# Loads of queries, keys and values one step later and in several pieces, with five buffers of attention outputs

## The chip, the cores and the metric

The kernel runs on one core of a Trainium2 chip. The metric is the device time of one execution in microseconds (us): lower is better. The time before is the median of three runs, 1153.46 us (1153.4 to 1158.42). The engines have their usual short names: PE is TensorE (matmul; PEld its weight loads), DVE is VectorE, ACT is ScalarE, POOL is GpSimd, SP is SyncE. SP computes nothing here: it issues DMA transfers, one after the other, in the order of the program.

## The reference

Two layers follow one another. The first is attention over 8 sequences of 576 positions with 8 heads of 64; each head sees only a causal band. Four heads see the last 32 positions, four see every fourth of the last 128. The second is a mixture of 8 experts over the 4608 tokens, of which each token takes the two with the highest noisy gate logits.

```
mask_plain = (rel >= 0) & (rel < window)
mask_dil = (rel >= 0) & (rel < window * dilation) & (rel % dilation == 0)
...
attn = attn / (np.sum(attn, axis=-1, keepdims=True) + 1e-09)
return np.matmul(attn, v)
...
noisy_logits = logits + noise_scale * noise
top2 = np.argpartition(-noisy_logits, 2, axis=1)[:, :2]
...
    h = np.maximum(x[mask] @ w1[e], 0.0)
    out[mask] += top2_w[mask, k, None] * (h @ w2[e])
```

All of it is float32. In the kernel the expert products are made of three matmuls on values that are split into a high and a low part.

## The kernel before, in words

**Attention.** The work is cut into 8 groups: four pairs of sequences, and for each pair first the four dilated heads, then the four plain ones. A group has three steps, so there are 24 steps (k = 0 to 23), and group g holds steps 3g, 3g+1 and 3g+2. The loop over i (line 879) is a software pipeline: in pass i it emits the scores of step i (`qk`), the exponential and the transpose of step i-1 (`expo`, `ptr`), the stores and transposes of the outputs of step i-2 (`store_x`, `x_transpose`), the product with the values of step i-1 (`pv`) and the gate matmuls of step i-2 (`gate_mm`).

`qk` needs the keys `KT` and queries `QT` of its group; `pv` needs its values, `VD` for dilated heads and `VP[0]`, `VP[1]` for plain ones. There is one set of these buffers for the dilated and one for the plain heads. The loads of group g+1's values can thus go out when group g-1 has used its own, those of group g+2's keys and queries when group g has.

`pv` ends in a VectorE multiply (line 354) that writes the normalized output `x` of its step, one of three buffers. `store_x` writes it to the scratch tensor `xs` in HBM with six DMAs (lines 365 and 367), from where the experts' gathers fetch it. A buffer of `x` can be written again when the stores that read it have landed.

**Order.** The order on each queue is that of the program text; nothing is reordered on the chip. What has no fixed place in the loop is hung into numbered slots: `at(kb, f)` puts `f` into slot kb, and pass i works off slot 2i (`fillers`, before `store_x`) and slot 2i+1 (after `pv` and `gate_mm`). So the lines that the change touches, 783 to 790, say behind which stores on SP's queue each load stands. Before, the values of group g+1 go to slots 6g+1 and 6g+2, and keys and queries of group g+2 to slot 6g+5, each tensor in one DMA. `VD` is loaded in three DMAs, `VP` in two, one for each sequence.

Other things that SP issues in these slots: two fills of the table `tab` (line 236, slots 6 and 12; it waits for VectorE), clears of the output (line 860, from slot 38 on), the loads of the first expert's w1 (line 565, from slot 41 on) and, for the first expert, small loads of the list of its tokens (line 611), which VectorE copies at line 627. The gate's selection (`gate`) is a generator that is worked off a few instructions at a time.

**Experts.** After the loop come the experts. For each, the tokens' rows are gathered from `xs` by GpSimd (line 643 or 650), transposed, split, and multiplied by w1 (line 697) and w2 (line 738); GpSimd adds the weighted rows to the output (line 715). Weights are staged through two buffers `ws` and split by ScalarE and VectorE (lines 573 to 588). Here `plan` places loads and splits by a reckoned time of TensorE. The first loads of w2 (line 579) are due at once, so they follow the last attention stores on SP's queue, and ScalarE splits the first piece (line 586) between the evictions of the first expert's hidden layer (line 701).

Of the kernel before, what the change touches and what calls it, by code (L numbers as in the profile page):

```python
# [9 lines left out]
F32 = mybir.dt.float32  # L10
# [35 lines left out]
def attention_moe_kernel(ctx, tc, qt, kp, kd, vpl, vdl, w_gate, w_noise, noise, w1, w2, out, CAP=1216, SPLITS=(0, 384, 896)):  # L46
# [25 lines left out]
    sm = actx.enter_context(tc.tile_pool(name="sm", bufs=2))  # L72
# [20 lines left out]
    def qk_loads(g, parts=1):  # L93
        u, ty = g // 2, 1 - g % 2
        for i in range(parts):
            for dst, src in ((KT[ty], (kp, kd)[ty][u]), (QT[ty], qt[u, ty])):
                n = dst.shape[1] // parts
                yield lambda d=dst[:, n * i:n * i + n], s=src[:, n * i:n * i + n]: sync.dma_start(d, s)

    def v_loads(g):  # L100
        u, ty = g // 2, 1 - g % 2
        if ty:
            d = VD.rearrange("p j h y c -> p (j h y c)")
            n = d.shape[1] // 3
            for i in range(3):
                yield lambda i=i: sync.dma_start(d[:, n * i:n * i + n], vdl[u, :, n * i:n * i + n])
        else:
            for b in range(2):
                yield lambda b=b: sync.dma_start(VP[b].rearrange("p j h c -> p (j h c)"), vpl[u, b])
# [138 lines left out]
    def micro(n=1):  # L248

        n = (1, n, 2 * n)[rate[0]]
        for g in list(gens):
            while n > 0 and g not in held:
                try:
                    r = next(g)
                except StopIteration:
                    gens.remove(g)
                    break
                n -= 1  # L260
                if r == 2:
                    room[0] -= 1
                if r == 1 or room[0] <= 0:
                    held.add(g)
                if r == 3:
                    break
# [6 lines left out]
    def blocks(st, ty):  # L273

        for r in range(6):
            for w in range(2):
                a, jp = divmod(r, 3)
                if ty == 0:
                    b, ub = divmod(12 * st + 2 * r + w, 18)
                else:  # L280
                    b, ub = divmod(6 * st + 2 * jp + w, 9)
                yield r, w, a, jp, b, ub
# [47 lines left out]
    def pv(k):  # L330
        g, st = divmod(k, 3)
        ty = 1 - g % 2
        pt = PT.pop(k)
        o = aps.tile([128, 2, 512], F32, name="o", tag="o")
        for hh in range(4):
            for r, w, a, jp, b, ub in blocks(st, ty):
                qd, c0 = (r, hh) if r < 4 else (2 * (r - 4) + hh // 2, 4 + hh % 2)
                if ty == 0:
                    y, src = hh // 2, 2 * (hh % 2) + a
                    rhs = VP[b][64 * w:64 * w + 64, ub // 2, hh]  # L340
                else:
                    y, src = a, hh
                    rhs = VD[64 * w:64 * w + 64, 3 * st + jp, hh, y]
                tensor.matmul(o[32 * qd:32 * qd + 32, w, 65 * c0:65 * c0 + 65],
                              lhsT=pt[64 * w:64 * w + 64, y, 128 * jp + 32 * src:128 * jp + 32 * src + 32],
                              rhs=rhs, start=True, stop=True, skip_group_check=True)
        ov = o[:, :, 0:390].rearrange("p w (c d) -> p w c d", d=65)
        x = sm.tile([128, 2, 6, 64], F32, name="x", bufs=3)
        den = sm.tile([128, 2, 6], F32, name="den")
        vector.tensor_scalar(den, ov[:, :, :, 64], 1e-9, None, op0=OP.add)  # L350
        micro(1)
        vector.reciprocal(den, den)
        micro(1)
        vector.tensor_tensor(x, ov[:, :, :, 0:64], den.unsqueeze(3).to_broadcast([128, 2, 6, 64]), op=OP.mult)
        XG[k] = x
# [408 lines left out]
    def plan(t, f, lag=None):  # L764

        if lag is not None:
            plan(t, lambda: plan(now[0] + lag, f()))
        else:
            heappush(due, (t, next(turn), f))
# [9 lines left out]
    def at(kb, *fs):  # L779
        fill.setdefault(kb, []).extend(fs)  # L780

    NK = 12 * U
    for g in range(2 * U):
        s0 = 6 * g
        if g + 1 < 2 * U:
            for i, f in enumerate(v_loads(g + 1)):
                at(s0 + 1 + i // 2, f)
        if g + 2 < 2 * U:
            for f in qk_loads(g + 2):
                at(s0 + 5, f)  # L790
    for u in range(U):
        for st in range(3):
            if (u, st) != (U - 1, 2):
# [67 lines left out]

    places = [*range(SL_ZERO, NK + 5)]
    for i in range(NZERO):
# [15 lines left out]
    for i in range(NS + 2):  # L879
        slot[0] = 2 * i  # L880
        early[0] = True
        micro(2)
        early[0] = False
        if i < NS:
            qk(i)
        micro(2)
        if 1 <= i <= NS:
            expo(i - 1)
        micro(2)
        if 1 <= i <= NS:  # L890
            ptr(i - 1)
        micro(2)
        micro(2)
        fillers(2 * i)
        if i >= 2:
            store_x(i - 2)
            x_transpose(i - 2)
        micro(2)
        if 1 <= i <= NS:
            pv(i - 1)  # L900
        micro(2)
        if i >= 2:
            gate_mm(i - 2)
        micro(2)
        micro(2)
        fillers(2 * i + 1)
# [24 lines left out]
    for kb in sorted(fill):  # L931
        for f in fill.pop(kb):
            plan(2.0 * (kb - NK - 5), f)
    start = 0.0
# [135 lines left out]
```

## Time and profile before

| what | value |
|---|---|
| median of 3 runs | 1153.46 us |
| profiled execution, its time | 1155.89 us |
| profiled execution, span from first to last instruction | 1154.2 us |
| TensorE busy (matmul) | 1023.6 us, 89% of the span |
| VectorE, ScalarE, GpSimd busy | 468.6, 289.4, 509.3 us |
| mean granted TensorE clock | 0.950 |
| last score matmul, last `pv` multiply | 243.0 us, 261.5 us |
| first and last store of `xs` | 18.8 us, 272.3 us |

The page cuts the span into 40 slices of 28.9 us. Attention fills the first nine of them. A row of a timeline gives the start, the duration, the engine (SPq is SP's queue), the line, the operation and the number of instructions merged into the row; in square brackets the engine's idle time ahead of it and what ended that. A DMA instruction's duration on SPq is the time until SP could hand it over, not that of the transfer. A row of waits gives the engine and line that waited, for what, and then the sum, the count and the longest, in us. A row of windows gives the busy time and instruction count of each of the five engines, the granted clock, the share of time in which the core's 16 DMA engines were busy, and what they moved in GB/s.

### The profile page before, as it was taken

How to read it: one execution, taken by the hardware profiler on the slowest of the kernel's cores; microseconds unless marked ns; L12 is line 12 of the kernel's file. 1: busy time of each engine (PE TensorE's matmuls, PEld its weight loads, DVE VectorE, ACT ScalarE, POOL GpSimd, SP SyncE). 2: the span in 40 equal slices, each digit the busy share in tenths (PEclk: the TensorE clock that was granted, in tenths of full speed). 3: DMA queues.
4: the chain of work that ended last, by engine and by line, in shares of the span. 5: the costliest groups of instructions: out<-in, count | busy, mean ns of one | idle time of the engine just before them, and what ended most of it. 6: DMA issues, size and time to landing. Idle time of an engine off the chain costs nothing. (4 is left out here: it accounts for less than half of the span.)

```text
span 1154.2 us, 22635 instructions
## 1 busy us (share of the span) xinstructions
PE 1023.6 (89%) x9630; PEld 870.0 (75%) x9631; DVE 468.6 (41%) x1043; ACT 289.4 (25%) x540; POOL 509.3 (44%) x620
## 2 busy tenths in 40 slices
PE   6765766455889999999999999999999999999996
PEld 4554545345669878897988899888978888998895
DVE  5544353444424454334433543444343335423221
ACT  1433332252212231213122322222231223212110
POOL 3000623242836676357534654463566256542112
PEclk8898877778999999999999999999999999999998
DMA  9665555655633443434342434333343524343123
GB/s 341 233 220 189 179 190 206 198 184 177 204 71 60 117 103 92 78 80 112 75 109 49 116 62 112 85 89 73 85 109 72 111 51 112 63 112 73 19 28 43
DMA packets 78538, 135.07 MB, mean 117 GB/s; under 512 B 29168, under 2 KB 41504, under 8 KB 75616
## 3 DMA queue, kind: packets, MB, share of 16 engines
q1 hardware_dynamic: 55520, 93.22, 24.5%
q0 software_dynamic: 22912, 40.35, 19.4%
q8 instruction: 77, 1.26, 0.4%
q14 instruction: 29, 0.24, 0.1%
HBM read 92.72 MB, written 40.81 MB: 116 GB/s over the span
## 5 line engine op out<-in xcount | busy, mean ns | idle before, releaser
L697 PE MATMUL up<-x,w1h 128*128 128x512 f32 (+2 forms) x1536 | 408.7, 350 | 0.0
L650 POOL DMA_INDIRECT g<-xs,ixi x266 | 266.3, 1001 | 94.7 <-issue 76.2
L697 PEld LDWEIGHTS up<-x,w1h 128*128 128x128 f32 x1536 | 276.8, 189 | 24.5 <-DVE hl L702 0.2
L697 PE MATMUL up<-x,w1l 128*128 128x384 f32 (+2 forms) x768 | 267.6, 348 | 0.0
L715 POOL DMA_INDIRECT out_rows<-y,ixs x70 | 112.1, 1602 | 311.3 <-DVE y L747 279.4
L738 PE MATMUL dn<-w2h,hh 128*128 128x512 f32 x576 | 225.3, 391 | 1.2 <-DVE y L747 1.2
L738 PE MATMUL dn<-w2h,hl 128*128 128x512 f32 x576 | 225.2, 391 | 0.0
L738 PE MATMUL dn<-w2l,hh 128*128 128x512 f32 x576 | 225.0, 391 | 0.0
L702 DVE SCALAR_TENSOR_TENSOR hl<-up,hh 128x384 fp32r<-128x384 f32 (+2 forms) x192 | 106.8, 557 | 238.8 <-ACT hh L701 238.8
L701 ACT ACTIVATE hh<-up 128x384 fp32r<-128x384 f32 (+2 forms) x192 | 96.7, 507 | 238.7 <-PE up L697 236.2
L697 PEld LDWEIGHTS up<-x,w1l 128*128 128x128 f32 x768 | 145.1, 189 | 12.5
L539 POOL DMA_INDIRECT tab<-en,si x72 | 71.0, 987 | 126.0 <-DVE lg L437 70.5
L738 PEld LDWEIGHTS dn<-w2h,hh 128*128 128x128 f32 x576 | 108.5, 188 | 23.6 <-DVE y L747 1.6
L738 PEld LDWEIGHTS dn<-w2h,hl 128*128 128x128 f32 x576 | 108.4, 188 | 22.7
L738 PEld LDWEIGHTS dn<-w2l,hh 128*128 128x128 f32 x576 | 108.4, 188 | 22.0
L747 DVE TENSOR_SCALAR y<-dn,ixs 128x512 f32<-128x512 f32 x63 | 47.1, 750 | 143.6 <-PE dn L738 143.6
L669 ACT CAST x<-xr 128x512 fp32r<-128x512 f32 x70 | 42.0, 599 | 200.1 <-DVE xr L667 200.1
L575 DVE TENSOR_TENSOR w1l<-ws,w1h 128x1024 fp32r<-128x1024 f32 x32 | 38.9, 1215 | 82.0 <-ACT w1h L573 82.0
L573 ACT CAST w1h<-ws 128x1024 fp32r<-128x1024 f32 x32 | 33.0, 1049 | 101.5 <-DMA ws<-in_moe_w 101.5
L303 PE MATMUL s<-kt,qt 64*32 64x64 f32 x2304 | 35.1, 238 | 22.1 <-issue 21.9
L303 PEld LDWEIGHTS s<-kt,qt 64*32 64x32 f32 x2304 | 28.3, 112 | 33.3 <-issue 32.6
L670 DVE TENSOR_TENSOR x<-xr,x 128x512 fp32r<-128x512 f32 x70 | 46.2, 661 | 17.5 <-ACT x L669 17.4
(152 smaller groups left out, 809.1 us busy)
## 6 DMA issues: line engine op xcount, KB each, us to landing
ws<-in_moe_w SPq DMA_DIRECT2D x64, 512.0 KB
out_rows<-zero SPq DMA_DIRECT2D x38, 256.0 KB
vd<-in_vdl SPq DMA_DIRECT2D x12, 780.0 KB
vp<-in_vpl SPq DMA_DIRECT2D x8, 1170.0 KB
qt<-in_qt SPq DMA_DIRECT2D x7, 1152.0 KB
xs<-x SPq DMA_DIRECT2D x48, 128.0 KB
kt<-in_kp SPq DMA_DIRECT2D x4, 1216.0 KB
g<-xs,ixi POOLq DMA_INDIRECT x266
```

Of the source, the lines that this page charges most:

```text
L303: tensor.matmul(s[32 * qd:32 * qd + 32, y, 64 * e:64 * e + 64], lhsT=QV[ty][64 * y:64 * y + 64, b, x, 32 * ub:32 * ub + 32], rhs=KV[ty][64 ...
L539: ins = gpsimd.indirect_dma_start(out=tab, out_offset=bass.IndirectOffsetOnAxis(ap=si[:, kq, t:t + 1], axis=0), in_=en[:, kq, t], in_offse ...
L575: return lambda: vector.tensor_tensor(b, s, a.bitcast(F32), op=OP.subtract)
L650: gpsimd.indirect_dma_start(out=g[:, j], out_offset=None, in_=xq, in_offset=bass.IndirectOffsetOnAxis(ap=IX[e][1][:, r0 // 32 + j:r0 // 32 ...
L669: scalar.copy(xh[:, :, o:o + rn], xr[:, :, 0:rn])
L670: return lambda: vector.tensor_tensor(xl[:, :, o:o + rn], xr[:, :, 0:rn], xh[:, :, o:o + rn].bitcast(F32), op=OP.subtract)
L697: tensor.matmul(p[:, 0:n], lhsT=a[:, 128 * f:128 * f + 128], rhs=b[:, kc, 0:n], start=(i == 0), stop=(i == 11))
L701: scalar.activation(hh[:, f, 0:n], p[:, 0:n], AF.Relu)
L702: vector.scalar_tensor_tensor(hl[:, f, 0:m], p[:, 0:m], 0.0, hh[:, f, 0:m].bitcast(F32), op0=OP.max, op1=OP.subtract)
L715: ins = gpsimd.indirect_dma_start(out=out, out_offset=bass.IndirectOffsetOnAxis(ap=sc[0:rn, t, 1:2], axis=0), in_=y[0:rn], in_offset=None, ...
L738: tensor.matmul(p[0:rn], lhsT=a[:, f, o:o + rn], rhs=b[:, f % 2], start=(i == 0), stop=(i == 23))
L747: vector.tensor_scalar(y[0:rn], p[0:rn], wsc, None, op0=OP.mult)
```

## The change

```
-        x = sm.tile([128, 2, 6, 64], F32, name="x", bufs=3)
+        x = sm.tile([128, 2, 6, 64], F32, name="x", bufs=5)
...
     for g in range(2 * U):
         s0 = 6 * g
         if g + 1 < 2 * U:
             for i, f in enumerate(v_loads(g + 1)):
-                at(s0 + 1 + i // 2, f)
+                at(s0 + 3 + 2 * i, f)
         if g + 2 < 2 * U:
-            for f in qk_loads(g + 2):
-                at(s0 + 5, f)
+            for i, f in enumerate(qk_loads(g + 2, 2)):
+                at(s0 + 7 + 2 * (i // 2), f)
```

The outputs `x` get five buffers instead of three. The pieces of the values of group g+1 go to slots 6g+3, 6g+5 and (for `VD`, which has three) 6g+7, one each, instead of all to 6g+1 and 6g+2. The keys and queries of group g+2 are cut into two halves, one for each sequence, so that there are four DMAs instead of two; the first half of keys and queries goes to slot 6g+7, the second to 6g+9, instead of all to 6g+5. All of these slots are odd: their loads stand behind the stores that the same pass issues. A piece is issued two to five slots (one to two and a half passes) later than before. The loads ahead of the loop (keys and queries of groups 0 and 1, values of group 0) are as they were. The same bytes are moved and the same arithmetic is done.

## The prediction

> **What bounds the kernel now.** I read the page's slices first: TensorE is busy nine tenths and more from slice 10 on, and six tenths or so before that. So the change, which touches only the attention loop (the first 262 us), can gain or lose in the early part only. There I read the waits, and the queue of SyncE (SP), which issues all loads and stores in program order.
>
> ```profile
> DVE x L354 <- DMA xs<-x: 40.8, 12, 7.8
> ...
> SPq L98 <- PE xtp L376: 1.3, 2, 0.7
> ```
>
> The first row is from the waits between 57 and 205 us: VectorE stands 40.8 us, in 12 places, at the multiply that writes `x`, until the stores of an old `x` have landed. The change aims at that row. The second is the longest wait that SP itself has between 40 and 239 us, 1.3 us in all: SP always has something to issue. What it issues in one period of three steps:
>
> ```profile
> 128.15 0.65 SPq L98 DMA_DIRECT2D kt<-in_kp  x1
> 128.84 0.43 SPq L98 DMA_DIRECT2D qt<-in_qt  x1
> 129.37 0.54 SPq L365 DMA_DIRECT2D xs<-x  x1
> 129.96 5.00 SPq L367 DMA_DIRECT2D xs<-x  x2
> ...
> 140.96 1.09 SPq L109 DMA_DIRECT2D vp<-in_vpl  x2
> 142.14 0.54 SPq L365 DMA_DIRECT2D xs<-x  x1
> 142.73 4.84 SPq L367 DMA_DIRECT2D xs<-x  x2
> ...
> 153.82 0.64 SPq L365 DMA_DIRECT2D xs<-x  x1
> ...
> 159.62 0.61 SPq L98 DMA_DIRECT2D kt<-in_kd  x1
> ```
>
> Columns: start, duration, what. From one pair of key and query loads to the next 159.62 - 128.15 = 31.5 us pass, without a hole. A step's six stores without a load ahead of them take 159.62 - 153.82 = 5.8 us; with the K and Q pair ahead 140.96 - 128.15 = 12.8 us, with the V pair 153.82 - 140.96 = 12.9 us. So each batch of loads costs the queue 7.0 us, and 3 x 5.8 + 2 x 7.0 = 31.4 us is the period. What the DMA engines do meanwhile (share and GB/s are the last columns):
>
> ```profile
> 130.50:135.00 4.50, 3.71 (x139) 2.77 (x137) 1.62 (x4) 1.37 (x3) 3.72 (x7) 1.00 0.98 391
> 150.50:159.00 8.50, 6.08 (x186) 4.44 (x172) 3.58 (x34) 2.83 (x7) 0.00 (x0) 0.57 0.22 68
> ```
>
> While a load drains they are full at 391 GB/s; while stores alone drain they are 0.22 busy at 68 GB/s. Loads and stores take turns, and the sum of both sets the pace. VectorE's wait for `xs` is the form in which that pace reaches the compute, not its cause. The end of the stretch says the same:
>
> ```profile
> 270.62 2.83 SPq L367 DMA_DIRECT2D xs<-x  x2
> 273.50 0.68 SPq L860 DMA_DIRECT2D out_rows<-zero  x1
> 274.28 0.94 SPq L579 DMA_DIRECT2D ws<-in_moe_w  x2
> ...
> 280.86 1.04 ACT L586 CAST w2h<-ws 128x1024 fp32r<-128x1024 f32 x1 [12.12 <-DMA ws<-in_moe_w]
> ...
> 284.17 0.22 PE L499 MATMUL posp<-ob,tri 128*128 128x48 bf16 x1 [9.85 <-DVE ob L491]
> ```
>
> The first load of w2 is issued at 274.28, right behind the last attention stores, and ScalarE waits 12.12 us for it, with ScalarE's ReLU evictions and then TensorE (9.85 us) queued behind. So the expert phase starts when the SP queue has worked off everything of the attention. **The time moves with the moment at which that w2 load lands**, 280.9 us.
>
> **The change part by part.** *Five buffers of `x`.* Step i's multiply then waits for the stores of five steps ago instead of three. This takes away VectorE's 40.8 us here, but adds no throughput to the queue. The stall goes to the next thing that is late: a load. K and Q now stand behind one (first half) and two (second half) more steps' stores, V behind one to three, so I expect TensorE to wait at the score matmuls (L303) of every third step, with the transposes, the P V matmuls and VectorE's maximum queued behind. Price: 0, covered by the queue's 31.5 us period; if the cover were gone it would be a gain (below).
>
> *Pieces.* Sizes from the page:
>
> ```profile
> vd<-in_vdl SPq DMA_DIRECT2D x12, 780.0 KB
> vp<-in_vpl SPq DMA_DIRECT2D x8, 1170.0 KB
> qt<-in_qt SPq DMA_DIRECT2D x7, 1152.0 KB
> kt<-in_kp SPq DMA_DIRECT2D x4, 1216.0 KB
> ```
>
> A K and Q pair is 2368 KB or 2.42 MB, at 391 GB/s 6.2 us; the V pair 2340 KB, 2.40 MB, 6.1 us. The measured 7.0 leaves 0.8 us that is not bytes. After the change the same bytes come in three batches per period, not two, and K and Q in four DMAs, not two: 12 more DMAs over the six later groups. Their issue (0.43 us for `qt` above, some 5 us in all if bare) lies inside the time in which SP is held back by a full queue anyway (the 5.00 and 4.84 us of L367). Whether 0.8 us belongs to a batch, to a DMA or to a byte, these rows don't show; I look at batches of other shapes:
>
> ```profile
> 172.54 1.59 SPq L106 DMA_DIRECT2D vd<-in_vdl  x3
> ...
> 185.31 0.63 SPq L365 DMA_DIRECT2D xs<-x  x1
> ...
> 218.91 1.00 SPq L860 DMA_DIRECT2D out_rows<-zero  x2
> ...
> 225.38 1.16 SPq L860 DMA_DIRECT2D out_rows<-zero  x2
> ```
>
> V in three DMAs and a step of stores take 185.31 - 172.54 = 12.8 us, no more than V in two, so a DMA more costs nothing. Two clears (0.52 MB, 1.3 us of bytes) and a step take 6.5 us, that is 0.7 over a bare step: small batches may even hide 0.6 us. Ends: 6 more batches at +0.8 (4.8 us lost), or all 0.8 us gone and 0.6 hidden per batch: 6 x (2 x 0.8 + 3 x 0.6) = 20 us gained. I take 0, between them, since the two shapes of V agree on a price per byte.
>
> [...]
>
> *One step later: the start.* This is where I find a price.
>
> ```profile
> 6.20 1.93 SPq L109 DMA_DIRECT2D vp<-in_vpl  x2
> 18.85 0.69 SPq L365 DMA_DIRECT2D xs<-x  x1
> ...
> 30.71 0.79 SPq L98 DMA_DIRECT2D kt<-in_kd  x1
> 31.55 0.43 SPq L98 DMA_DIRECT2D qt<-in_qt  x1
> 36.84 0.35 SPq L236 DMA_DIRECT2D tab<-free  x1
> 37.24 0.54 SPq L365 DMA_DIRECT2D xs<-x  x1
> ...
> 1.00:28.00 27.00, 18.00 (x476) 11.45 (x477) 14.41 (x49) 5.17 (x7) 10.47 (x24) 0.87 0.99 352
> ...
> 36.80:40.00 3.20, 2.00 (x40) 1.02 (x40) 1.35 (x3) 0.62 (x4) 0.00 (x0) 0.73 0.98 382
> ```
>
> The first loads fill the engines to 28 us, both halves of VP among them. SP waits 4.9 us, to 36.84, for VectorE's table fill (L236), and under that wait K and Q of group 2 run: no hole (0.98 busy to 40, next to the last column). After the change the second half of VP goes behind step 0's stores, and K and Q of group 2 move past the L236 wait and step 1's stores. The engines then have: first loads to 28 - 3.1 = 25 us (1170 KB less), stores of step 0 to 31, VP's half to 34, and nothing until 37. So 2.8 us of queue time are lost, and work moved behind the hole is paid later. Ends: 0, if less traffic lets VectorE reach the fill as much earlier; 6.4 us, all of that K and Q pair (1280 + 1152 KB), if the stores and VP are done sooner. I take 2.8.
>
> *One step later: the last groups.* K and Q of group 7 (second half) and its V, 1.2 + 2.4 MB or 9.2 us, move behind the index load L611.
>
> ```profile
> 218.26 0.61 SPq L611 DMA_DIRECT2D ixf<-tab  x1
> ...
> 222.72 0.16 DVE L627 TENSOR_SCALAR ixh<-ixf 128x6 int32<-128x6 int32 x1 [13.29 <-DMA ixf<-tab]
> ...
> 226.59 0.51 SPq L565 DMA_DIRECT2D ws<-in_moe_w  x1
> ...
> 234.55 1.04 ACT L573 CAST w1h<-ws 128x1024 fp32r<-128x1024 f32 x1 [6.08 <-DMA ws<-in_moe_w]
> ```
>
> VectorE's 13.29 us there shrink: the index lands 9.2 - 2.8 = 6.4 us earlier, at 216. But these loads now stand ahead of the first w1 load (226.59), for which ScalarE already waits 6.08 us; all loads are ahead of it in both orders, so it lands 2.8 us later than 234.5, and ScalarE's wait grows by what VectorE's lost. From there on the queue's content is unchanged. They also pass the clears at L860 and step 17's stores; score and P V matmuls of group 7 read them two steps later, some 21 us at 10.5 a step, against 7 us of batch.
>
> **Sum.** -40.8 (VectorE) + 40.8 (same pace, other waits) + 0 (pieces) + 2.8 (hole at 34 us) - 6.4 + 6.4 (index, then w1) = +2.8 us. The profiled execution took 1155.9 us for a span of 1154.2, and gives 1158.7; it stood 2.4 us above the median of the runs, so against that median: 1153.5 + 2.8 = 1156.3.
>
> **Rivals.** *Slower: each batch or DMA has a fixed price.* 0.8 us x 6 batches (0.4 x 12 DMAs is the same) + 2.8 = +7.6: 1161. It decides from 0.5 us a batch on. For it: the 0.8 us over the bytes. Against: V in three pieces.
> *Faster: smaller batches overlap the stores.* The bytes' own price alone, 6 x 2 x 0.8 = 9.6 us gained, less 2.8: 1147; with the 0.6 us of hiding too, 1136. For it: the two clears, and 0.22 busy engines beside stores. Against: for 2.4 MB nothing was hidden in six periods. [...]
> *Faster: the wait for `x` is itself the bound.* Then 40.8 us come back: 1113. Against it: SP has no hole for the compute to fill.
> *The change does little:* the same stalls under other names, 1153.5.
>
> **Numbers.** Forecast 0.46, slower rival 0.25, overlap 0.21, waits returned 0.03, nothing 0.05. A measurement tells about 0.5% (5.8 us) from no change. Faster: overlap (1147 and 1136) and returned waits, 0.24. Slower: its rival and a sliver of the forecast's upper end, 0.26. Same: the rest, 0.50. The forecast's own range is 1153.5 to 1160; to leave out no more than 2 in 10 I go up past the slower rival to 1163 and down past the nearer overlap case to 1144.
>
> **What would show it.** Right: SP's issues remain gapless from 60 to 205 us with three steps in about 31 us, `DVE x <- xs` falls under 5 us and TensorE's or VectorE's waits on loads take its place; a hole before L236; L627 near 216 us; `ws` of w1 and of w2 2 to 3 us later than 234.5 and 280.9. Wrong: three steps in under 30 us (overlap) or over 32 us (fixed price), or a w2 load that lands before 278.

## The result, and the profile after

| | before | after |
|---|---|---|
| median of 4 runs each, taken together | 1155.41 us (1153.4 to 1158.42) | 1168.43 us (1164.67 to 1171.89) |
| ratio, 95% interval | | 1.011 [1.0068, 1.0152] |
| profiled execution: time, span | 1155.89, 1154.2 us | 1168.47, 1166.8 us |
| TensorE busy, mean granted clock | 1023.6 us, 0.950 | 1027.7 us, 0.941 |

The ratio is worked out from the executions in the undisturbed, fast state alone and can differ a little from the ratio of the medians, here and below. The change costs 13 us. The forecast was 1156.3, its range ended at 1163: the sign was in doubt, the size was wrong, and even the slower rival (1161) was too low.

VectorE's wait for old stores is gone, as forecast. Waits of the changed kernel between 57 and 205 us (engine and line, what it waited for; sum in us, count, longest):

```profile
DVE mx L310 <- PE s L303: 51.1, 14, 10.8
...
PE s L303 <- DMA qt<-in_qt: 21.5, 5, 9.8
...
DVE x L354 <- DMA xs<-x: 0.4, 1, 0.4
```

The 40.8 us at line 354 are now 0.4. TensorE waits 21.5 us for queries instead, and VectorE's maximum waits 51.1 us for the scores behind it. The same view of the kernel before, which has no wait for queries:

```profile
DVE mx L310 <- PE s L303: 20.2, 8, 5.2
```

So VectorE got back 40.4 us at line 354 and lost 30.9 us at line 310. Nothing of it reaches the end, because the end is set elsewhere. The end of the attention in the changed kernel, first on SP's queue, then on VectorE, then on ScalarE (start, duration; idle time ahead and its cause in brackets):

```profile
221.44 0.58 SPq L611 DMA_DIRECT2D ixf<-tab  x1
...
238.88 0.74 SPq L565 DMA_DIRECT2D ws<-in_moe_w  x1
...
286.82 1.14 SPq L579 DMA_DIRECT2D ws<-in_moe_w  x2
```

```profile
225.88 0.16 DVE L627 TENSOR_SCALAR ixh<-ixf 128x6 int32<-128x6 int32 x1 [13.15 <-DMA ixf<-tab]
```

```profile
249.35 1.04 ACT L573 CAST w1h<-ws 128x1024 fp32r<-128x1024 f32 x1 [17.70 <-DMA ws<-in_moe_w]
...
293.44 1.04 ACT L586 CAST w2h<-ws 128x1024 fp32r<-128x1024 f32 x1 [10.25 <-DMA ws<-in_moe_w]
```

The load of w2 is issued at 286.82 instead of 274.28, and ScalarE starts on it at 293.44 instead of 280.86: 12.58 us later. The profiled time grew by 1168.47 - 1155.89 = 12.58 us. From that cast to the end of the span it takes 1166.8 - 293.4 = 873.4 us, before 1154.2 - 280.9 = 873.3. So all that was lost was lost ahead of this load, and it is SP's queue that issues it. Two places show where.

**The hole at 34 us.** SP's queue of the changed kernel:

```profile
27.81 0.59 SPq L109 DMA_DIRECT2D vp<-in_vpl  x1
39.89 0.35 SPq L236 DMA_DIRECT2D tab<-free  x1
40.29 0.54 SPq L365 DMA_DIRECT2D xs<-x  x1
```

SP now stands from 28.4 to 39.9 us before the table fill (to 36.84 before). Windows of the same stretch (five engines' busy time and count, the clock, and as the last two columns the DMA engines' share and GB/s):

```profile
32.00:34.00 2.00, 0.00 (x0) 0.00 (x0) 0.31 (x1) 0.00 (x0) 0.00 (x0) 1.00 0.34 116
34.00:36.00 2.00, 1.08 (x42) 0.99 (x43) 0.40 (x1) 0.00 (x0) 0.00 (x0) 0.89 0.07 28
36.00:38.00 2.00, 2.00 (x11) 1.91 (x9) 1.73 (x4) 0.87 (x2) 0.00 (x0) 0.50 0.04 8
38.00:40.00 2.00, 2.00 (x110) 1.67 (x112) 1.96 (x9) 0.79 (x2) 0.00 (x0) 0.76 0.00 0
```

From 34 to 40 us the DMA engines are all but idle; before, they moved 382 GB/s at 37 to 40 us. The prediction has the engines empty from 34 us on. They are already two thirds idle between 32 and 34 us, because SP had handed over step 0's stores by 27.8 us and not by 31; and the fill came at 39.9 us, not at 36.8. The hole is longer at both ends, more at its end.

**The pace of the loop.** Seven rows of the changed kernel's queue, each the first load behind one step's stores; no load lies in between except those named below:

```profile
112.49 0.60 SPq L98 DMA_DIRECT2D kt<-in_kd  x1
...
121.96 0.59 SPq L98 DMA_DIRECT2D kt<-in_kd  x1
...
133.43 0.61 SPq L106 DMA_DIRECT2D vd<-in_vdl  x1
...
142.02 0.60 SPq L106 DMA_DIRECT2D vd<-in_vdl  x1
...
154.13 0.60 SPq L98 DMA_DIRECT2D kt<-in_kp  x1
...
166.68 0.61 SPq L109 DMA_DIRECT2D vp<-in_vpl  x1
...
176.39 0.66 SPq L98 DMA_DIRECT2D kt<-in_kd  x1
```

From these, with the bytes at 391 GB/s and 5.8 us for a step's six stores, as in the prediction:

| from | loads in the batch | bytes, us | stores, us | sum | measured | more |
|---|---|---|---|---|---|---|
| 112.49 | K, Q half (640 + 576 KB) | 3.2 | 5.8 | 9.0 | 9.5 | 0.5 |
| 121.96 | K, Q half, V (780 KB) | 5.2 | 5.8 | 11.0 | 11.5 | 0.5 |
| 133.43 | V (780 KB) | 2.0 | 5.8 | 7.8 | 8.6 | 0.8 |
| 142.02 | V (780), K, Q half (608 + 576) | 5.1 | 5.8 | 10.9 | 12.1 | 1.2 |
| 154.13 | K, Q half, V (1170 KB) | 6.2 | 5.8 | 12.0 | 12.6 | 0.6 |
| 166.68 | V (1170 KB) | 3.1 | 5.8 | 8.9 | 9.7 | 0.8 |

Before, a batch of 2.4 MB cost 0.8 us over its bytes. Now batches of a third to all of that cost 0.5 to 1.2, on average 0.7, and the smallest cost no less than the largest: the price goes with the batch, not with the byte. The six differ by a factor of two and say no more than that. And there are three of them in a period, not two.

### The profile page after: what moved, and what is told of

It is laid out like the page before. It is cut to its first block, busy times and chain, and to the rows that moved or that the text cites. A ratio compares the mean times of both kernels' runs of the same rounds, so it can differ in the third digit from the quotient of the medians.

```text
span 1166.8 us, 22651 instructions
## 1 busy us (share of the span) xinstructions
PE 1027.7 (88%) x9630; PEld 873.2 (75%) x9631; DVE 470.0 (40%) x1043; ACT 288.9 (25%) x540; POOL 508.5 (44%) x620
## 5 line engine op out<-in xcount | busy, mean ns | idle before, releaser
L697 PEld LDWEIGHTS up<-x,w1l 128*128 128x128 f32 x768 | 145.5, 189 | 12.6
L667 DVE STREAM_TRANSPOSE xr<-g 128x512 f32<-128x512 f32 x70 | 47.3, 676 | 16.1 <-DMA g<-xs,ixi 16.1
```

Source lines behind the costliest of these rows:

```text
L667: vector.transpose(xr[:, :, 0:rn].rearrange("p c (g t) -> p g c t", t=32), g[:, 0:n].rearrange("p g (c d) -> p g c d", d=32))
L697: tensor.matmul(p[:, 0:n], lhsT=a[:, 128 * f:128 * f + 128], rhs=b[:, kc, 0:n], start=(i == 0), stop=(i == 11))
```

## The experiments

Every kernel below computes the whole reference. The first four ran on the same chip as the result, side by side. The others fell on other chips, where the kernel before itself takes 1231 to 1247 us; each is compared only with the kernel before on its own chip.

**Which part costs the time? Four kernels that split the change.** The late-load theory holds the waits of TensorE for K and Q responsible, the buffer theory the five buffers, the queue theory the hole plus the batches.

*Loads alone, three buffers:* the change with

```
-        x = sm.tile([128, 2, 6, 64], F32, name="x", bufs=5)
+        x = sm.tile([128, 2, 6, 64], F32, name="x", bufs=3)
```

> The loads in their new places and pieces, x still with three buffers. Queue theory (SP's queue sets the pace; the loss is a hole in it near 31 to 40 us, some 8 us, and some 0.9 us more per period of three steps, together 12): +12 us against the kernel before, as the whole change. Late-load theory (the loss is TensorE's 28.3 us of waits for queries that come too late): +13 or more, since the waits for x come on top. Buffer theory (five buffers let the compute run ahead and SP fall behind): near 0.

*Buffers alone:* the kernel before with

```
-        x = sm.tile([128, 2, 6, 64], F32, name="x", bufs=3)
+        x = sm.tile([128, 2, 6, 64], F32, name="x", bufs=5)
```

> The kernel before with five buffers of x and nothing else. Queue theory: 0, within 2 us; VectorE's 42.8 us of waits for the stores turn into waits for something else. Late-load theory: 5 to 20 us faster, because no load is late and the waits for x are gone. Buffer theory: +12.

*The change, but group 0's turn (values of group 1, keys and queries of group 2) as before:*

```
+        old = g == 0
...
-                at(s0 + 3 + 2 * i, f)
+                at(s0 + 1 + i // 2 if old else s0 + 3 + 2 * i, f)
...
-            for i, f in enumerate(qk_loads(g + 2, 2)):
-                at(s0 + 7 + 2 * (i // 2), f)
+            for i, f in enumerate(qk_loads(g + 2, 1 if old else 2)):
+                at(s0 + 5 if old else s0 + 7 + 2 * (i // 2), f)
```

> The whole change, except that the loads of the first group's turn (values of group 1, keys and queries of group 2) stay where and as they were. Queue theory: the hole before the table fill (line 236) is gone, and of 12 to 13 us some 8 are regained: +4 to +5. Late-load theory: one of six waits for queries is gone: +10 to +11. Buffer theory: +12.

*Group 0's turn alone as after, all else as before:* the same lines with

```
+        old = g != 0
```

and three buffers.

> The kernel before, with only the loads of the first group's turn (values of group 1, keys and queries of group 2) moved and cut as in the change; all later loads and the three buffers of x as before. Queue theory: the hole alone, +8. Late-load theory: +2. Buffer theory: 0.

| kernel | median (before 1155.06) | ratio, 95% | w2's cast starts | span | from cast to end |
|---|---|---|---|---|---|
| before (profile shown above) | | 1 | 280.9 | 1154.2 | 873.3 |
| the change (profile after) | | 1.011 | 293.4 | 1166.8 | 873.4 |
| loads alone | 1168.93 | 1.0121 [1.0102, 1.0139] | 293.2 | 1166.8 | 873.6 |
| buffers alone | 1154.61 | 0.9999 [0.9986, 1.0012] | 277.9 | 1150.9 | 873.0 |
| start as before | 1162.07 | 1.0062 [1.0043, 1.0081] | 285.9 | 1160.9 | 875.0 |
| start alone | 1161.49 | 1.0057 [1.0041, 1.0073] | 285.0 | 1158.2 | 873.2 |

The buffers cost and bring nothing. The start alone costs 1161.49 - 1155.06 = 6.4 us, the rest alone 1162.07 - 1155.06 = 7.0, together 13.4 against 13.9 for all loads: the parts add up, which fits a queue that is worked off in order. The queue theory expected a part of it in each, but not in these sizes: +8 for the start, +4 to +5 for the rest. The buffer theory falls with the second kernel, the late-load theory with the third and fourth, which it had placed the other way round (the first, +13.9, fits it as well as the queue theory). The last column is the strongest reading: over five of the six kernels it stays within 0.6 us while the span moves by 16. Even the 3 us by which the buffers' profiled execution is shorter than the profile of before lie ahead of this one load. They also say how far a single profile's cast can be trusted: these two kernels take the same time, and their casts start 2.9 us apart. The cast's rows in the profiles of loads alone, buffers alone, start as before and start alone, in this order:

```profile
293.19 1.04 ACT L586 CAST w2h<-ws 128x1024 fp32r<-128x1024 f32 x1 [11.43 <-DMA ws<-in_moe_w]
```

```profile
277.92 1.04 ACT L586 CAST w2h<-ws 128x1024 fp32r<-128x1024 f32 x1 [10.97 <-DMA ws<-in_moe_w]
```

```profile
285.90 1.04 ACT L586 CAST w2h<-ws 128x1024 fp32r<-128x1024 f32 x1 [13.97 <-DMA ws<-in_moe_w]
```

```profile
284.98 1.04 ACT L586 CAST w2h<-ws 128x1024 fp32r<-128x1024 f32 x1 [7.88 <-DMA ws<-in_moe_w]
```

Why does the fill come later than before? TensorE in the profile of before, the scores of step 3:

```profile
30.77 1.75 PE L303 MATMUL s<-kt,qt 64*32 64x64 f32 x96
```

of the changed kernel, TensorE and then VectorE:

```profile
30.12 0.79 PE L303 MATMUL s<-kt,qt 64*32 64x64 f32 x57
34.92 0.64 PE L303 MATMUL s<-kt,qt 64*32 64x64 f32 x39 [4.01 <-issue]
```

```profile
35.60 0.96 DVE L310 TENSOR_REDUCE mx<-s 128x12 f32<-128x768 f32 x1 [3.30 <-PE s L303]
...
39.53 0.29 DVE L235 TENSOR_SCALAR free<-free 128x146 int32<-128x146 int32 x1
```

After 57 of 96 score matmuls TensorE stands 4.0 us, with no semaphore or transfer to account for it ("issue"). VectorE's maximum of step 3 follows at 35.60, then its instructions for the table, whose last one starts at 39.53; SP's fill waits for that. In the kernel before the same last instruction starts at 36.49: VectorE is 3.0 us later, and so is the fill (39.89 against 36.84). TensorE has such a stand there too, but three rows of work later, where the fill no longer depends on it:

```profile
38.01 0.50 PE L344 MATMUL o<-vd,pt 64*32 64x65 f32 x20 [2.72 <-issue]
```

In the start-alone kernel the stand is 3.83 us and the fill comes at 40.10; with the start as before there is no stand in these scores, and the fill comes at 36.56:

```profile
40.10 0.35 SPq L236 DMA_DIRECT2D tab<-free  x1
```

```profile
36.56 0.35 SPq L236 DMA_DIRECT2D tab<-free  x1
```

All four kernels with the moved start stand 3.8 to 4.0 us after the same 57 matmuls. Of the others some do not stand there and some do for up to 1.6 us, buffers alone among them, whose fill comes at 38.44:

```profile
33.47 0.64 PE L303 MATMUL s<-kt,qt 64*32 64x64 f32 x39 [1.36 <-issue]
```

The trace shows one thing more about these stands. It lists a DMA queue that it calls "instruction", with 77 packets of 16 KB in an execution. In the six profiles of the first chip TensorE has 71 stands of 1 us or more with the cause "issue" up to the end of the attention, and each ends 1.1 to 1.8 us after such a packet has landed. In the changed kernel no packet runs on that queue between 27.0 and 32.7 us; then comes one (the queue's packets, MB and share between 32.6 and 33.7 us), which lands at 33.6, and TensorE goes on at 34.92:

```profile
q8 instruction: 1, 0.02, 5.3%
```

In the kernel before, that packet runs from 29.3 to 30.4 us, ahead of the scores. In the four kernels with the moved start it begins at 32.3 to 32.7 us, in before, in buffers alone and with the start as before at 29.3 to 30.8. So TensorE most likely stood for its instructions, and they came late. In the changed kernel the moved half of `VP`, which SP handed over at 27.81, keeps the DMA engines full from 30 to 32 us at 412 GB/s, and the packet begins when they are free; that it queued behind this load is likely but not shown, since no view has the moment at which it was asked for.

**Is it the pieces, or the later place?** *Keys and queries in halves, in their old slots, three buffers:*

```
-            for f in qk_loads(g + 2):
+            for f in qk_loads(g + 2, 2):
                 at(s0 + 5, f)
```

> The kernel before with keys and queries cut into halves, but issued in their old place; three buffers of x. Price-per-DMA theory (each of 12 more DMAs costs the queue 0.4 us): +5 us. Price-per-batch theory (each batch of loads between two steps' stores costs 0.8 us beside its bytes; here there are as many batches as before): 0. Tail theory (the loss that is left without the hole, 7 us, comes from the last groups' loads, which now stand just ahead of the first w1 load): 0.

> As the earlier run of this kernel (keys and queries in halves, issued in their old place), whose chip fed instructions so slowly that TensorE stood some 20 us at a time and the queue was not the bound. Where the queue is the bound: price per DMA: +5 us; price per batch: 0; tail theory: 0.

*Later, but uncut (group 0's turn as before, five buffers):* each group's values all to slot 6g+3, keys and queries whole to 6g+7.

```
+                at(s0 + 1 + i // 2 if old else s0 + 3, f)
...
+            for f in qk_loads(g + 2):
+                at(s0 + 5 if old else s0 + 7, f)
```

> The first turn's loads as before; all later loads one step later, but uncut and each pair at once (values at slot 6g+3, keys and queries at slot 6g+7); five buffers of x. Price-per-batch theory: as many batches as before, 0 to +1. Price-per-DMA theory: 0. Tail theory: the values of group 7 (2.4 MB) still stand behind the index load and just ahead of the first w1 load: +4 to +7.

> As the earlier run of this kernel (first turn as before, all later loads one step later but uncut), on a chip where the queue is the bound. Price per batch or per DMA: 0 to +1 us. Tail theory: +4 to +7.

> First turn as before, all later loads one step later but uncut. Where the queue is the bound: price per batch or per DMA 0 to +1 us; tail theory +4 to +7. Otherwise 0, within 4.

> First turn as before, all later loads one step later but uncut. Where the queue is the bound: price per batch or per DMA 0 to +1 us; tail theory +4 to +7. On a chip that starves TensorE of instructions: 0, within 3.

*Cut and later, but the first turn and the last ones as before:* the start-as-before kernel with

```
-        old = g == 0
+        old = g == 0 or g >= 5
```

> The whole change, except that the loads of the first group's turn and those of groups 6 and 7 that the last two turns issue (values of 6 and 7, keys and queries of 7) stay where and as they were. Of the 7 us that were left with the first turn as before: price-per-batch or per-DMA theory: two thirds stay, +4 to +5. Tail theory: all back, 0 to +1.

> As the earlier run of this kernel (first turn's and last two turns' loads as before, the rest as in the change), on a chip where the queue is the bound. Price per batch or per DMA: +4 to +5 us. Tail theory: 0 to +1.

> First turn's and last two turns' loads as before, the rest as in the change. Where the queue is the bound: price per batch or per DMA +4 to +5 us; tail theory 0 to +1. Otherwise 0, within 4.

> First turn's and last two turns' loads as before, the rest as in the change. Where the queue is the bound: price per batch or per DMA +4 to +5 us; tail theory 0 to +1. On a chip that starves TensorE of instructions: 3 to 5 us faster, as before.

| kernel | ratios with 95% intervals, one for each repetition |
|---|---|
| halves in place | 0.9999 [0.9973, 1.0024]; 1.0022 [0.9989, 1.0055] |
| later, uncut | 1.0011 [0.9989, 1.0032]; 0.9981 [0.9947, 1.0014]; 0.9989 [0.9956, 1.0022]; 0.998 [0.995, 1.0011] |
| cut and later, ends as before | 0.9968 [0.9942, 0.9994]; 0.9975 [0.9937, 1.0013]; 0.9965 [0.9935, 0.9995]; 0.9979 [0.9953, 1.0004] |

In time these tell nothing apart: on these chips, by the next experiment, SP's queue is not what sets the pace. The kernel that was to lose by its batches is if anything 0.3% faster. But the queue's rows can still be read: in both kernels shown next, SP itself waits at most 0.6 us for any one thing between 70 and 136 us. A load is compared with the like load, because in the cut kernels the first half of a plain group's keys stands behind a piece of values and that of a dilated group does not. From the first K load of group 3 to that of group 5, both plain and two periods apart, in later uncut and in cut and later (the last repetition of each):

```profile
70.25 0.55 SPq L98 DMA_DIRECT2D kt<-in_kp  x1
...
132.68 0.60 SPq L98 DMA_DIRECT2D kt<-in_kp  x1
```

```profile
71.72 0.38 SPq L98 DMA_DIRECT2D kt<-in_kp  x1
...
136.32 0.38 SPq L98 DMA_DIRECT2D kt<-in_kp  x1
```

Uncut takes 132.68 - 70.25 = 62.4 us (62.3 to 62.8 over four repetitions), cut 136.32 - 71.72 = 64.6 (63.8 to 65.4). On the chip of the result, two periods from plain group 5 to 7 take 191.16 - 128.15 = 63.0 us in the kernel before, of which this is the later row:

```profile
191.16 0.60 SPq L98 DMA_DIRECT2D kt<-in_kp  x1
```

In the change they take 207.97 - 142.72 = 65.3 us:

```profile
142.72 0.38 SPq L98 DMA_DIRECT2D kt<-in_kp  x1
...
207.97 0.38 SPq L98 DMA_DIRECT2D kt<-in_kp  x1
```

With the start as before, groups 3 to 5 take 134.34 - 70.43 = 63.9 us:

```profile
70.43 0.38 SPq L98 DMA_DIRECT2D kt<-in_kp  x1
...
134.34 1.03 SPq L98 DMA_DIRECT2D kt<-in_kp  x1
```

So being later costs the queue nothing, and one batch more in each period costs it (63.9 - 63.0) / 2 = 0.5 to (65.3 - 63.0) / 2 = 1.2 us. Halves that stay in one batch show no price; here from group 3's load to group 6's, in the second repetition:

```profile
62.68 0.61 SPq L98 DMA_DIRECT2D kt<-in_kp  x1
...
157.52 0.60 SPq L98 DMA_DIRECT2D kt<-in_kd  x1
```

These 94.8 us (96.7 in the first repetition) hold the second table fill as well, which in before lies between the same loads and makes them 96.3 us; six more DMAs at 0.4 us would have added 2.4. By the queue's rows the price is therefore that of a batch between two sets of stores, not that of a DMA.

Are the 7 us of the start-as-before kernel lost batch by batch, or at the last groups? Its later loads let SP reach the same stores earlier. The first stores of steps 5 and 17 in before, and then with the start as before:

```profile
79.38 0.54 SPq L365 DMA_DIRECT2D xs<-x  x1
...
206.18 0.54 SPq L365 DMA_DIRECT2D xs<-x  x1
```

```profile
71.38 0.54 SPq L365 DMA_DIRECT2D xs<-x  x1
...
201.13 0.54 SPq L365 DMA_DIRECT2D xs<-x  x1
```

Both steps have the same place in the order of loads, but the lead shrinks from 8.0 to 5.1 us in these four periods, 0.7 us a period, before the values of group 7 are issued, which the tail theory blames. The change loses 4.0 us on the same stretch and loads alone 2.6; buffers alone loses 0.6 and start alone gains 2.1. That speaks for the batches and against the tail as the whole of it. No timed run on a chip whose bound is the queue separates the two, so how much of the 7 us is batches stays open.

**Is the loss still there on such a chip? The change itself again.**

> The whole change once more, beside the kernels below on the same chip. Where the queue is the bound: +12 to +14 us. On a chip where TensorE stands for its instructions 20 us at a time: the queue catches up in those stands, and the loss falls to 0 to +5 us.

1248.71 us against 1246.43, ratio 0.9996 [0.9963, 1.0029]: there the change costs nothing that can be told, at most 3.6 us by the interval. One of its waits up to 300 us, and a window in the attention:

```profile
PE s L303 <- issue: 50.3, 41, 3.8
```

```profile
120.00:140.00 20.00, 4.37 (x59) 2.31 (x60) 0.00 (x0) 0.00 (x0) 14.79 (x30) 0.50 0.57 183
```

The same window in the profile of before on the first chip:

```profile
120.00:140.00 20.00, 16.37 (x571) 12.48 (x569) 8.05 (x15) 7.76 (x17) 14.88 (x30) 0.91 0.53 173
```

In these 20 us TensorE gets 59 matmuls instead of 571, 44 of them in the first 1.5 us, at half the clock; no semaphore and no transfer that the trace shows holds them up. It is not quite the stand of the first chip: no packet runs on the instruction queue from 116.7 to 142.5 us, and yet single matmuls come. The expert phase is longer too: from w2's cast to the end 1243.5 - 311.4 = 932.1 us, not 873. That the queue's 13 us find cover where TensorE itself is starved of instructions fits these rows, but no profile of the kernel before was taken on that chip, so it is argued and not shown.

**Can the stores be made cheaper?** In the kernel before, each of the two narrow stores (line 367) is cut in two by rows:

```
             for r in range(4, 6):
-                sync.dma_start(dst[r].rearrange("q (c d) -> c q d", c=2),
-                               x[64 * r - 256:64 * r - 192, w, 4:6].rearrange("p h d -> p (h d)"))
+                for c in range(2):
+                    p0 = 64 * r - 256 + 32 * c
+                    sync.dma_start(dst[r][:, 128 * c:128 * c + 128],
+                                   x[p0:p0 + 32, w, 4:6].rearrange("p h d -> p (h d)"))
```

The Trainium skill (DMA: Bandwidth & Descriptors, "Why a DMA increments its semaphore by 16 and not by 1") has the number of engines of a DMA go by the slowest dimension of its two sides: 2 in the old form (`c`), 16 in the new one (32 rows).

> The kernel before; only the narrow stores of line 367 are cut, each into two of 32 rows by 512 bytes, so that a step has ten store DMAs, not six. If the stores' price is that a DMA with an outer dimension of 2 keeps only two DMA engines busy (the page's rule), a bare step falls from 5.8 us of queue to some 4 us and the time by 15 to 35 us. If the price is SP's issue, 8 more DMAs per two steps at some 0.5 us make it 20 to 45 us slower. The queue theory as such fits either: the time must move with the queue.

> As the earlier run of this kernel (the kernel before with the narrow stores of line 367 cut in two), on a chip where the queue is the bound. Narrow stores keep few DMA engines busy: 15 to 35 us faster. Price in SP's issue: 20 to 45 us slower. On the other chip it was 0.8% faster.

> The kernel before with the narrow stores of line 367 cut in two. Where the queue is the bound, and if narrow stores keep few DMA engines busy: 10 to 35 us faster, more than the 0.7 to 0.8% of the two slower chips. Otherwise some 9 us faster.

1221.64 against 1231.46 us, 0.9921 [0.9892, 0.995]; 1240.35 against 1246.93, 0.993 [0.9898, 0.9962]; 1243.17 against 1246.43, 0.9952 [0.9926, 0.9977]. It is faster than the kernel before each time, by 0.5 to 0.8%, less than the 15 to 35 us that more engines were to bring. The sign that was named with them did not come either. From a step's first store to the next load, with no load in between, the first repetition takes 95.01 - 88.94 = 6.1 us:

```profile
88.94 0.51 SPq L365 DMA_DIRECT2D xs<-x  x1
...
95.01 0.36 SPq L98 DMA_DIRECT2D kt<-in_kd  x1
```

The others take 6.9 and 5.9, where some 4 was expected and the kernel before has 5.8. So what makes this kernel faster is open. It was measured only on chips where the queue is not the bound; the change itself ran on one of them.

## Why the prediction was wrong

- **SP's queue sets the end, through the w2 load: right, and more exactly than argued.** From that load's cast to the end it is 873.0 to 873.6 us in before, in the change and in three of the four parts. The queue also has no hole between 45 and 205 us, as forecast: what SP waits longest for between 40 and 239 us is 0.9 us in all.
- **Five buffers, -40.8 + 40.8 = 0: right.** 0.9999 alone, where TensorE waits 17.8 us for queries that come no later than before. The stall went where it was said to go, to the scores at line 303 and VectorE behind them. The rival "waits returned" (1113) is dead: 40.4 us of waits went away and no time came back.
- **The hole, +2.8: the mechanism right, the term mis-sized; 6.4 measured.** The step that failed is "nothing until 37": it took the fill to come at its old time. It came 3.0 us later, because step 3's scores were held up, most likely for TensorE's instructions. The bounds asked only whether the fill comes earlier or the transfers end sooner. They did end sooner, by some 1.5 us, but the stated end of 6.4 was reached mainly by the other road, and by luck.
- **Pieces, 0: wrong; +7.0 in time for all that is not the start, some +5 by w2's load.** The step that failed is the choice "a price per byte". The slower rival's 6 x 0.8 = 4.8 is near what w2's cast shows in the start-as-before kernel, 285.90 - 280.86 = 5.0 us later, and the queue's rows give 0.5 to 1.2 us for each added batch. The choice leaned on V in three DMAs against two. That shows that a DMA costs nothing, as the halves in place bear out; but those three DMAs are one batch, and the change makes more batches. The clears, the only small batches that it read, cost less than their bytes and gave no sign of a price. The mark for a fixed price had been set at three steps in over 32 us; the change takes 32.0 (63.9 / 2, from 112.49 to 176.39) to 32.6 (65.3 / 2).
- **Last groups, -6.4 + 6.4 = 0: right where the hole is away.** With the start as before, the index is read at 216.0 and w1's cast takes over the wait:

```profile
216.04 0.16 DVE L627 TENSOR_SCALAR ixh<-ixf 128x6 int32<-128x6 int32 x1 [13.25 <-DMA ixf<-tab]
```

```profile
238.70 1.04 ACT L573 CAST w1h<-ws 128x1024 fp32r<-128x1024 f32 x1 [16.91 <-DMA ws<-in_moe_w]
```

  6.7 us were gained at line 627 against before, and ScalarE's wait for w1 grew from 6.08 to 16.91 us. In the change itself the hole and the batches eat the gain, and line 627 comes at 225.9.
- **Sum.** 0 + 5 + 6.4 + 0 = 11.4 of the 13.4 that the two parts measure, with one term from a profile and one from times. By time alone it is 7.0 + 6.4. By w2's casts alone it is 5.0 + 4.1 (start alone, 284.98), against 12.6 for the change; single profiles of equal kernels differ by 2.9 us there, so the casts place the loss but do not size it. Of the start-as-before kernel's 7.0 us some 1.7 lie behind the cast (875.0 against 873.3), in one profile; what they are stays open. So does why a batch costs 0.7 us: loads and stores were not seen apart on single DMA engines.
- **A misreading without effect.** The page's slices show TensorE at nine tenths from the thirteenth slice on, not from the tenth.

## What to carry to other kernels

On a queue that issues loads and stores in order, count the batches of loads between the stores beside their bytes, not the DMAs: each turn from stores to loads and back cost some 0.7 us here, for batches of 0.8 to 2.4 MB alike. Before moving a load past a wait, ask what ran under that wait, and let the wait end later as well as earlier in the bounds: the loads that covered it were worth 6.4 us. If one transfer's landing fixes the rest to within a microsecond, as it did in five kernels of six here, look at that landing for every edit, over several executions; a stall removed elsewhere may only be renamed.

## What the runs showed of the hardware that was not expected

The same kernel takes 1155 us on one chip and 1231 to 1247 us on others. In the profile of the change on one of the slower ones, TensorE is handed 15 matmuls from 122.3 to 140.7 us, one in 1.2 us, with no wait that the trace names and at a clock of 0.50. A change worth 1.1% on the first chip is worth nothing that can be told there (0.9996 [0.9963, 1.0029]), so this ratio holds for the chip on which it was measured.

On the first chip TensorE's stands without a named cause look like waits for its instructions: 71 of 71 end 1.1 to 1.8 us after a packet of the instruction queue has landed, and 4.0 us of such a stand moved the table fill, and with it the whole queue.
